# Attention and two expert layers on one core: pooling moved from GpSimd to VectorE, half tiles merged into whole ones

## The chip, the cores and the metric

The kernel runs on one core of one Trainium2 chip. A core has five engines that run at the same time, each through a list of its own in a fixed order: TensorE (PE) multiplies matrices, VectorE (DVE), ScalarE (ACT) and GpSimd (POOL) work elementwise, and SyncE (SP) issues transfers. Engines wait for each other by semaphores. PSUM is the memory that TensorE writes its products to: eight banks, of 512 float32 numbers in each of 128 partitions. SBUF is the working memory. The metric is the device time of one execution, in microseconds (us), lower is better.

## What is computed

Attention whose keys and values are averaged over groups of eight tokens, then a layer of eight experts of which each token uses one, then a second such layer with a capacity for each expert. The part that the change touches, with B = 4, H = 8, S = 576, D = 64:

```
k_p = k.reshape(B, H, Sp, pool, D).mean(axis=3)       # pool = 8, Sp = 72
v_p = v.reshape(B, H, Sp, pool, D).mean(axis=3)
scores = scale * np.matmul(q, k_p.transpose(0, 1, 3, 2))
scores = scores - np.max(scores, axis=-1, keepdims=True)
attn = np.exp(scores)
attn = attn / (np.sum(attn, axis=-1, keepdims=True) + 1e-09)
out = np.matmul(attn, v_p)                            # the tokens x of the expert layers
logits = x @ w_gate + modality_bias[modality_id]      # argmax picks the expert, softmax its weight
h = np.maximum(x[mask] @ w1[e], 0.0)                  # for each expert e
out[mask] = gate_w[mask, None] * (h @ w2[e])
```

## The kernel before

The kernel has two stages on the time line. The attention stage makes the 2304 tokens in 18 tiles of 128 tokens, nine for each of two pairs of batches, and sends each finished tile to DRAM (xs). The expert stage then gathers tokens window by window and runs the two expert layers; it is bound by products on TensorE, and the change leaves it as it is.

All orders are written by hand: each engine runs its instructions in the order in which the program text issues them. The attention stage is the loop over i at L1197. Iteration i issues, in this order: `e_trans(i-1)` (L1000, TensorE turns the exponentials of tile i-1, ScalarE copies them out as eT), `scores(i+1)` (L972), the list `steps[i]`, `exps(i+1)` (L996, ScalarE), and `values(i-1)` (L1010). Each engine therefore has the pieces of three tiles in flight, but in a fixed order.

`scores` multiplies queries and pooled keys into two PSUM tiles `sc` of four heads each; VectorE takes the row maximum of each half (L988) and subtracts it from each half (L993, into exs). `values` multiplies the turned exponentials and the pooled values into two PSUM tiles `pv`, one for each half of the heads; VectorE then makes the reciprocals rs (L1019, L1022) and scales each half into the token tile xt (L1026) and the partial logits lgh (L1030). psc and psv are pools of two one-bank buffers each, so the products of the next tile can begin on a half when VectorE has read that half.

Between these instructions stand calls of `slot()`, which issue one waiting small step of VectorE from the list `pending`: mostly the gating of three finished tiles (L164, L1034).

`steps[i]` is filled by `turn(i, ...)` (L1120): preparation for later tiles. `pool_k` and `pool_v` (L888, L891) sum eight rows of keys or values. A pair has nine blocks of 128 pooled rows, in three groups of 4, 1 and 4 blocks (GR at L843). Groups 0 and 1 of pair 0 are summed on VectorE by one reduction for two blocks (L876); all other groups are summed on GpSimd by a tree of three additions (L881, L882, L886), issued at turns 0 to 3, 8 and 9. `k_cols`, `v_cols` and `v_rows` then bring the sums into the layouts kbd and vaug, through TensorE and with copies on ScalarE and VectorE (L944, L945). `biases` (L141), 14 small VectorE instructions from L143 to L156, stands in turn 2.

In iterations 12 to 15 the class `known` (L449) prepares the first window of the first expert layer ahead of time: `choose` and `hot` (L475, L494) rank tokens and make one-hot places, `others` (L511) sums up. For the first layer these run on GpSimd (`self.eng`), for the second on VectorE. VectorE also splits the first weights there (L209).

Loads of q, k and v are issued by SP in a fixed order (L1083 to L1095 and turn 2); buffers of `kin4` and `vin4` exist twice, so the last group of a pair waits until the sums of an earlier group have been read.

Of the kernel before, what the change touches and what calls it, by code (L numbers as in the profile page):

```python
# [69 lines left out]
def build(tc, A, out):  # L70
# [378 lines left out]
    class known:  # L449
# [5 lines left out]
        def __init__(self, m, e):  # L455
            self.m, self.T = m, (T1 // 2, T2)[m - 1]
            self.g, self.e = gs[m - 1], e
            self.hs = {}
            self.eng = (G, V)[m - 1]
# [15 lines left out]
        def choose(self):  # L475

            eng = self.eng
            r, u, one = (self.part(t) for t in (kt.rk[:, :, 0], kt.rk[:, :, 1], kt.ohu[:, :, 0]))
            dn, tmp, lt, place, ohv = (self.part(t) for t in (kt.dn, kt.tmp, kt.lt, kt.place, kt.ohv))
            eng.tensor_scalar(lt, r, 128.0, None, ALU.is_ge)  # L480
            eng.tensor_scalar(place, lt, -128.0, None, ALU.mult)
            eng.tensor_tensor(place, place, r, ALU.add)
            if self.m == 2:
                eng.tensor_tensor(tmp, r, u, ALU.add)
                eng.tensor_scalar(tmp, tmp, cap, None, ALU.is_lt)
                eng.tensor_tensor(dn, tmp, one, ALU.mult)
                one = dn
            eng.tensor_scalar(tmp, r, 256.0, None, ALU.is_lt)
            eng.tensor_tensor(dn, tmp, one, ALU.mult)
            eng.tensor_tensor(tmp, dn, self.part(C(f"id{self.m}")), ALU.mult)  # L490
            eng.tensor_tensor(ohv[:, :, 1], tmp, lt, ALU.mult)
            eng.tensor_tensor(ohv[:, :, 0], tmp, ohv[:, :, 1], ALU.subtract)
# [18 lines left out]
        def others(self):  # L511
# [5 lines left out]
            self.eng.tensor_scalar(self.part(kt.offp), kt.rk[:, 0:T, 0], kt.count, -1.0, ALU.min, ALU.mult)  # L517
            self.eng.tensor_scalar(self.part(kt.offp), self.part(kt.offp), 256.0, None, ALU.add)
            self.eng.tensor_scalar(kt.count, kt.count, -1.0, 256.0, ALU.mult, ALU.add)
            self.eng.tensor_scalar(kt.more, isgs[self.m - 1], kt.count, None, ALU.mult)  # L520
            self.eng.tensor_scalar(self.part(kt.shut), dn, 64.0, None, ALU.mult)
            if T < T2:
                self.eng.tensor_copy(kt.offp[:, T:], kt.count.to_broadcast([128, T2 - T]))
                self.eng.memset(kt.shut[:, T:], 0.0)
# [294 lines left out]
    with ExitStack() as es:  # L819
# [46 lines left out]
        def pool_rows(src, dst, pair, g, eng):  # L866
# [6 lines left out]
            if eng is V:  # L873
                for i, j in [(i, min(i + 2, n)) for i in range(0, n, 2)]:
                    u = o[:, i:j, 0] if dst is kps else o[:, i:j]
                    V.tensor_reduce(u, s[:, i:j].rearrange("p t (r d) -> p t d r", r=POOL), AX.X, ALU.add)  # L876
                    if dst is kps:
                        V.tensor_copy(o[:, i:j, 1], u)
                return
            t = ld.tile([128, 4, m], F32, name="tree")[:, 0:n]  # L880
            eng.tensor_tensor(t, s[:, :, 0:m], s[:, :, m : 2 * m], ALU.add)  # L881
            eng.tensor_tensor(t[:, :, 0 : m // 2], t[:, :, 0 : m // 2], t[:, :, m // 2 : m], ALU.add)  # L882
            a, z = t[:, :, 0:D], t[:, :, D : 2 * D]
            if dst is kps:
                a, z = bc(a, 2, [128, n, 2, D]), bc(z, 2, [128, n, 2, D])
            eng.tensor_tensor(o, a, z, ALU.add)  # L886

        def pool_k(pair, g, eng):  # L888
            pool_rows(kin, kps, pair, g, eng)

        def pool_v(pair, g, eng):  # L891
            pool_rows(vin, vps, pair, g, eng)
# [59 lines left out]
        pending = []  # L952

        def slot():
            if pending:
                pending.pop(0)()

# [15 lines left out]
        def scores(tile_):  # L973
            pair, i = divmod(tile_, 9)
            ex = exs[tile_ % 3][:, 0 : H * SK].rearrange("p (h g) -> p h g", h=H)
            scs, mxs = [], []
            for half in range(2):
                sc = psc.tile([128, 4, SK], F32, name="sc")
                for j in range(2):
                    c = 2 * half + j  # L980
                    for p0, n, b in parts(tile_):
                        if i < 8:
                            q = qT[pair, i % 4][:, c, i // 4, :, :]
                        else:
                            q = qT[pair, 4][:, c, b % 2, 0, :]
                        mm(sc[p0 : p0 + n, 2 * j : 2 * j + 2, :], q, kbd[b][:, c, :], start=True, stop=True)
                mx = at.tile([128, 4], F32, name=f"mx{half}")
                V.tensor_reduce(mx, sc, AX.X, ALU.max)  # L988
                slot()
                scs.append(sc)  # L990
                mxs.append(mx)
            for half in range(2):
                V.tensor_tensor(ex[:, 4 * half : 4 * half + 4, :], scs[half], bc(mxs[half], 2, [128, 4, SK]), ALU.subtract)  # L993
                slot()
# [15 lines left out]
        def values(tile_, eT, x, lgh):  # L1010
            rs = at.tile([128, H], F32, name="rs")
            pvs = []
            for half in range(2):
                pv = psv.tile([128, 4, VA], F32, name="pv")
                for j in range(3):
                    for p0, n, b in parts(tile_):
                        mm(pv[p0 : p0 + n, j : j + 2, :], eT[:, 3 * half + j, p0 : p0 + n], vaug[b][:, half, j],  # L1017
                           start=(j == 0), stop=(j == 2), skip_group_check=True)
                V.tensor_scalar(rs[:, 4 * half : 4 * half + 4], pv[:, :, D + E], float(POOL), POOL * 1e-9, ALU.mult, ALU.add)  # L1019
                pvs.append(pv)  # L1020
            slot()
            V.reciprocal(rs, rs)  # L1022
            slot()
            for half in range(2):
                hs = slice(4 * half, 4 * half + 4)
                V.tensor_tensor(  # L1026
                    x[:, 0:DM].rearrange("p (h d) -> p h d", h=H)[:, hs, :],
                    pvs[half][:, :, 0:D], bc(rs[:, hs], 2, [128, 4, D]), ALU.mult)
                slot()
                V.tensor_tensor(lgh[:, hs, :], pvs[half][:, :, D : D + E], bc(rs[:, hs], 2, [128, 4, E]), ALU.mult)  # L1030
# [69 lines left out]
        for g in range(2):  # L1100
            pool_k(0, g, V)
# [41 lines left out]
        turn(0, pool_k, 0, 2, G)  # L1143
        turn(1, pool_v, 0, 2, G)
# [4 lines left out]
        for g in range(2):  # L1149
            turn(2, pool_k, 1, g, G)  # L1150
# [186 lines left out]
```

## Time and profile before

| | |
|---|---|
| median of 3 runs | 653.54 us (650.95 to 657.12) |
| profiled execution: its time | 657.79 us |
| profiled execution: its span | 656.0 us |
| TensorE busy | 593.5 us, 90% of the span |
| VectorE busy | 411.2 us, 63% |
| ScalarE busy | 224.8 us, 34% |
| GpSimd busy | 149.6 us, 23% |
| end of the attention stage (first product of the expert stage) | 126.97 us |
| TensorE granted clock, mean | 0.955 |

The span is what the trace covers; about 1.8 us of the execution's time lie around it. The attention stage is some 127 us of it. A busy share is a mean over stages, so the attention stage is read apart in what follows. [...] "Idle before" in a row names what the engine's next instruction waited for. A row of the time line that merges several instructions gives the start of the first and the time until the end of the last.

### The profile page before, as it was taken

How to read it: one execution, taken by the hardware profiler on the slowest of the kernel's cores; microseconds unless marked ns; L12 is line 12 of the kernel's file. 1: busy time of each engine (PE TensorE's matmuls, PEld its weight loads, DVE VectorE, ACT ScalarE, POOL GpSimd, SP SyncE). 2: the span in 40 equal slices, each digit the busy share in tenths (PEclk: the TensorE clock that was granted, in tenths of full speed). 3: DMA queues.
4: the chain of work that ended last, by engine and by line, in shares of the span. 5: the costliest groups of instructions: out<-in, count | busy, mean ns of one | idle time of the engine just before them, and what ended most of it. 6: DMA issues, size and time to landing. Idle time of an engine off the chain costs nothing. (4 is left out here: it accounts for less than half of the span.)

```text
span 656.0 us, 11642 instructions
## 1 busy us (share of the span) xinstructions
PE 593.5 (90%) x3990; PEld 531.2 (81%) x3990; DVE 411.2 (63%) x1100; ACT 224.8 (34%) x395; POOL 149.6 (23%) x149
## 2 busy tenths in 40 slices
PE   7767998889889999999999989998889999999990
PEld 4666988879788899898888878996778999988980
DVE  4689769797656867787678576227776561228110
ACT  3432674223112122112136432136663361236210
POOL 1197006012012022012113312222221212123200
PEclk8788999799979999999999989999999999999995
DMA  9997687168551022011018302926766854121110
GB/s 237 243 282 184 208 271 231 50 195 284 222 204 43 29 67 68 18 50 68 24 47 265 113 19 91 298 69 195 260 234 240 279 184 148 50 68 42 45 25 23
DMA packets 57594, 93.04 MB, mean 142 GB/s; under 512 B 6265, under 2 KB 31097, under 8 KB 57332
## 3 DMA queue, kind: packets, MB, share of 16 engines
q1 hardware_dynamic: 50084, 68.69, 33.8%
q0 software_dynamic: 7360, 22.77, 10.8%
q8 instruction: 57, 0.93, 0.6%
q14 instruction: 77, 0.63, 0.3%
q10 hardware_dynamic: 16, 0.02, 0.0%
HBM read 68.22 MB, written 24.89 MB: 142 GB/s over the span
## 5 line engine op out<-in xcount | busy, mean ns | idle before, releaser
L438 PE MATMUL py<-h,hh 128*128 128x512 f32 x296 | 119.5, 404 | 5.4 <-ACT hh L428 3.3
L398 PE MATMUL first<-xT,h 128*128 128x256 f32 x480 | 121.4, 285 | 1.4 <-issue 1.4
L399 PE MATMUL first<-xT,l 128*128 128x256 f32 x480 | 119.4, 281 | 3.2 <-issue 2.0
L439 PE MATMUL py<-l,hh 128*128 128x512 f32 x296 | 116.8, 394 | 2.2 <-DVE l L209 2.2
L440 PE MATMUL py<-h,hl 128*128 128x512 f32 x296 | 116.8, 395 | 0.0
L405 ACT ACTIVATE hh<-first 128x512 fp32r<-128x512 f32 x64 | 38.3, 598 | 211.7 <-PE first L401 196.5
L406 DVE SCALAR_TENSOR_TENSOR hl<-first,hh 128x512 fp32r<-128x512 f32 x64 | 44.2, 690 | 105.7 <-ACT hh L405 47.8
L398 PEld LDWEIGHTS first<-xT,h 128*128 128x128 f32 x480 | 91.0, 189 | 5.1 <-issue 3.6
L399 PEld LDWEIGHTS first<-xT,l 128*128 128x128 f32 x480 | 91.0, 189 | 3.5 <-DVE l L209 1.9
L209 DVE TENSOR_TENSOR l<-rr,h 128x1024 fp32r<-128x1024 f32 x72 | 83.8, 1221 | 3.4 <-ACT h L205 3.0
L736 DVE SCALAR_TENSOR_TENSOR junk<-y,wg2b 128x512 bf16<-128x512 f32 x112 | 77.3, 690 | 3.4
L401 PE MATMUL first<-xT,h 128*128 128x256 f32 x480 | 76.6, 281 | 0.0
L438 PEld LDWEIGHTS py<-h,hh 128*128 128x128 f32 x296 | 55.7, 188 | 17.9 <-ACT hh L428 6.0
L440 PEld LDWEIGHTS py<-h,hl 128*128 128x128 f32 x296 | 55.7, 188 | 13.5 <-DVE hl L413 1.1
L439 PEld LDWEIGHTS py<-l,hh 128*128 128x128 f32 x296 | 55.8, 189 | 13.0 <-DVE l L209 3.1
L401 PEld LDWEIGHTS first<-xT,h 128*128 128x128 f32 x480 | 65.5, 189 | 0.0
L205 ACT CAST h<-rr 128x1024 fp32r<-128x1024 f32 x64 | 62.8, 1044 | 2.1 <-issue 2.1
L377 POOL DMA_INDIRECT out<-y,ids x18 | 24.5, 1361 | 160.4 <-ACT y L605 107.5
L779 POOL DMA_INDIRECT ys<-y,tok x20 | 20.3, 1016 | 173.2 <-DVE y L774 101.9
L1017 PE MATMUL pv<-vaug,eT 96*128 96x146 f32 (+1 forms) x240 | 35.2, 323 | 11.6 <-DVE lgh L1030 11.6
L1017 PEld LDWEIGHTS pv<-vaug,eT 96*128 96x128 f32 (+1 forms) x240 | 32.1, 204 | 13.4 <-issue 8.8
L605 ACT ACTIVATE y<-py,xg 128x512 f32<-128x512 f32 x35 | 24.0, 686 | 38.9 <-PE py L440 28.7
(272 smaller groups left out, 888.5 us busy)
## 6 DMA issues: line engine op xcount, KB each, us to landing
rr<-in_moe_w SPq DMA_DIRECT2D x72, 512.0 KB, 6.0
ys<-zero SPq DMA_DIRECT2D x18, 260.0 KB, 6.8
xs<-xt SPq DMA_DIRECT2D x36, 130.0 KB, 2.4
out<-zero SPq DMA_DIRECT2D x1, 4608.0 KB
kin<-in_k SPq DMA_DIRECT2D x3, 1024.0 KB, 5.7
vin<-in_v SPq DMA_DIRECT2D x3, 1024.0 KB, 7.9
qin<-in_q SPq DMA_DIRECT2D x4, 512.0 KB, 11.7
wg2b<-wgd SPq DMA_DIRECT2D x1, 2048.0 KB
```

Of the source, the lines that this page charges most:

```text
L205: copy(hi[q], raw[q])
L209: eng.tensor_tensor(lo[q], raw[q], hi[q].bitcast(F32), ALU.subtract)
L398: mm(g[:, j, :], h1[q][:, c, fs], hi, start=(c == 0), stop=False)
L399: mm(g[:, j, :], l1[q][:, c, fs], hi, start=False, stop=False)
L401: mm(g[:, j, :], h1[q][:, c, fs], xT[:, c, :, 1, :], start=False, stop=(c == CH - 1))
L405: ACT.activation(hh, g, AF.Relu)
L406: V.scalar_tensor_tensor(hl, g, 0.0, hh.bitcast(F32), ALU.max, ALU.subtract)
L438: mm(py[t], hh[:, j, :], h2[q][:, j, :], start=st, stop=False)
L439: mm(py[t], hh[:, j, :], l2[q][:, j, :], start=False, stop=False)
L440: mm(py[t], hl[:, j, :], h2[q][:, j, :], start=False, stop=sp)
L736: V.scalar_tensor_tensor(junk, self.y[:, t, 0:DM], 1.0, wg2b[:, e, :], ALU.mult, ALU.mult, accum_out=self.lg[:, t, e : e + 1])
L1017: mm(pv[p0 : p0 + n, j : j + 2, :], eT[:, 3 * half + j, p0 : p0 + n], vaug[b][:, half, j], start=(j == 0), stop=(j == 2), skip_group_check ...
```

## The change

Three things change; none touches the expert stage, except that the preparation for its first window is issued on another engine.

1. `pool_rows` always runs on VectorE, by the tree of three additions, on two blocks at a time, with a `slot()` between pieces. The groups that GpSimd summed at turns 0, 1, 2, 3, 8, 9 are now summed on VectorE at turns 1, 2, 4, 5, 8, 9. Groups 0 and 1 of pair 0 use the tree too, where they used the reduction.
2. `scores` and `values` use one two-bank PSUM tile for both halves, and one VectorE instruction where there were two (maximum, subtraction, rs, xt, lgh). psc and psv have one such buffer each, so they take as many banks as before.
3. `choose`, `hot` and `others` of the first expert layer run on VectorE. On GpSimd only memsets and indirect transfers are left.

```diff
-            self.eng = (G, V)[m - 1]
...
-            if self.m == 1:
-                return [lambda t=t: G.tensor_scalar(self.ohp[:, t, :], iota, place[:, t : t + 1], None, ALU.is_equal) for t in range(T)]
-            return [lambda t=t: hot_places(self.ohp, place, t, 6) for t in range(0, T, 6)]
+            return [lambda t=t: hot_places(self.ohp, place, t, min(6, T - t)) for t in range(0, T, 6)]
...
-        psc = es.enter_context(tc.tile_pool(name="psc", bufs=2, space=PSUM))
+        psc = es.enter_context(tc.tile_pool(name="psc", bufs=1, space=PSUM))
...
-        psv = es.enter_context(tc.tile_pool(name="psv", bufs=2, space=PSUM))
+        psv = es.enter_context(tc.tile_pool(name="psv", bufs=1, space=PSUM))
...
+            for i, j in [(i, min(i + 2, n)) for i in range(0, n, 2)]:
+                t = ld.tile([128, 2, m], F32, name="tree", bufs=2)[:, 0 : j - i]
+                V.tensor_tensor(t, s[:, i:j, 0:m], s[:, i:j, m : 2 * m], ALU.add)
+                V.tensor_tensor(t[:, :, 0 : m // 2], t[:, :, 0 : m // 2], t[:, :, m // 2 : m], ALU.add)
+                a, z = t[:, :, 0:D], t[:, :, D : 2 * D]
+                if dst is kps:
+                    a, z = bc(a, 2, [128, j - i, 2, D]), bc(z, 2, [128, j - i, 2, D])
+                V.tensor_tensor(o[:, i:j], a, z, ALU.add)
+                if j < n:
+                    slot()
...
+            sc = psc.tile([128, 2, 512], F32, name="sc")[:, :, 0 : 4 * SK].rearrange("p a (h g) -> p a h g", h=4)
...
+            mx = at.tile([128, 2, 4], F32, name="mx")
+            V.tensor_reduce(mx, sc, AX.X, ALU.max)
+            slot()
+            V.tensor_tensor(ex, sc, bc(mx, 3, [128, 2, 4, SK]), ALU.subtract)
+            slot()
+            slot()
...
             slot()
+            V.tensor_scalar(rs, pv[:, :, :, D + E], float(POOL), POOL * 1e-9, ALU.mult, ALU.add)
             V.reciprocal(rs, rs)
             slot()
+            V.tensor_tensor(x[:, 0:DM].rearrange("p (a h d) -> p a h d", a=2, h=4),
+                            pv[:, :, :, 0:D], bc(rs, 3, [128, 2, 4, D]), ALU.mult)
+            slot()
+            V.tensor_tensor(lgh.rearrange("p (a h) e -> p a h e", a=2), pv[:, :, :, D : D + E], bc(rs, 3, [128, 2, 4, E]), ALU.mult)
+            slot()
...
-        turn(0, pool_k, 0, 2, G)
-        turn(1, pool_v, 0, 2, G)
+        turn(1, pool_k, 0, 2)
+        turn(2, pool_v, 0, 2)
...
-            turn(2, pool_k, 1, g, G)
-            turn(3, pool_v, 1, g, G)
+            turn(4, pool_k, 1, g)
+            turn(5, pool_v, 1, g)
...
-        turn(8, pool_k, 1, 2, G)
-        turn(9, pool_v, 1, 2, G)
+        turn(8, pool_k, 1, 2)
+        turn(9, pool_v, 1, 2)
```

The remaining lines of the diff write V for `eng` and `self.eng`, and drop the engine from the calls.

How the change moves instructions is seen in the lists of two engines. In the rows, a number behind a name is that of the buffer; line numbers of the changed kernel differ by up to 16. First VectorE from the end of tile 2's scores to the start of `biases`, before: tile 0's values (rs to lgh), then tile 3's scores.

```order
L1019 TENSOR_SCALAR rs<-pv 128x4 x2
L1022 RECIPROCAL rs<-rs 128x8
L1026 TENSOR_TENSOR xt<-pv,rs 128x256
L1030 TENSOR_TENSOR lgh<-pv,rs 128x32
L1026 TENSOR_TENSOR xt<-pv,rs 128x256
L1030 TENSOR_TENSOR lgh<-pv,rs 128x32
L988 TENSOR_REDUCE mx_423<-sc 128x4
L988 TENSOR_REDUCE mx_428<-sc 128x4
L993 TENSOR_TENSOR exs_154<-sc,mx_423 128x288
L993 TENSOR_TENSOR exs_154<-sc,mx_428 128x288
```

The same place of VectorE in the changed kernel, from the second of two equal pieces of three additions:

```order
L877 TENSOR_TENSOR tree<-kin_195 128x512
L878 TENSOR_TENSOR tree<-tree 128x2x128
L882 TENSOR_TENSOR kps<-tree 128x256
L1007 TENSOR_SCALAR rs<-pv 128x8
L1008 RECIPROCAL rs<-rs 128x8
L1010 TENSOR_TENSOR xt<-pv,rs 128x512
L1013 TENSOR_TENSOR lgh<-pv,rs 128x64
L978 TENSOR_REDUCE mx<-sc 128x8
L980 TENSOR_TENSOR exs_154<-sc,mx 128x576
```

Six additions of the last group of keys of pair 0 now stand ahead of tile 0's values, and ten instructions on halves have become six. The other groups come in the same way: `pool_v` of this group behind `biases`, and four more pairs of pieces in iterations 4, 5, 8 and 9.

The second place is VectorE in iteration 12, between tile 13's scores and tile 11's values. Before:

```order
L993 TENSOR_TENSOR exs_155<-sc,mx_1208 128x288
L993 TENSOR_TENSOR exs_155<-sc,mx_1213 128x288
L473 COPY rk<-pm 128x10
L1019 TENSOR_SCALAR rs<-pv 128x4 x2
L1022 RECIPROCAL rs<-rs 128x8
L1026 TENSOR_TENSOR xt<-pv,rs 128x256
```

The same place of VectorE in the changed kernel:

```order
L472 COPY rk<-pm 128x10
L478 TENSOR_SCALAR lt_k<-rk 128x9
L479 TENSOR_SCALAR place_k<-lt_k 128x9
L480 TENSOR_TENSOR place_k<-place_k,rk 128x9
L486 TENSOR_SCALAR tmp_k<-rk 128x9
L487 TENSOR_TENSOR dn<-tmp_k,ohu 128x9
L488 TENSOR_TENSOR tmp_k<-dn,cb 128x9
L489 TENSOR_TENSOR ohv_k<-tmp_k,lt_k 128x9
L490 TENSOR_TENSOR ohv_k<-tmp_k,ohv_k 128x9
L227 TENSOR_TENSOR ohp<-cb,place_k 128x768
L227 TENSOR_TENSOR ohp<-cb,place_k 128x384
L1007 TENSOR_SCALAR rs<-pv 128x8
```

Eight small instructions of `choose` and two of `hot` now stand ahead of tile 11's values; before they were 17 instructions on GpSimd. In iteration 15 seven instructions of `others` move over in the same way.

## Rows read from the trace of the kernel before

**Rows 1.** First line of the page.
```profile
span 656.0 us, 11642 instructions
```

**Rows 2.** Five stretches: start:end, length, busy us of PE, PEld, DVE, ACT, POOL; PEclk, DMA share, GB/s.
```profile
0.00:30.20 30.20, 21.09 (x87) 14.74 (x88) 16.61 (x29) 10.43 (x23) 2.49 (x9) 0.79 0.94 232
30.20:67.00 36.80, 26.57 (x175) 25.15 (x175) 32.60 (x95) 14.06 (x33) 30.66 (x24) 0.82 0.94 239
67.00:94.00 27.00, 26.39 (x227) 24.77 (x227) 20.63 (x95) 18.83 (x44) 0.00 (x0) 0.97 0.70 221
94.00:119.70 25.70, 20.64 (x185) 19.12 (x184) 23.48 (x95) 13.94 (x27) 13.11 (x27) 1.00 0.67 218
119.70:127.00 7.30, 7.29 (x43) 6.55 (x43) 2.81 (x16) 0.95 (x2) 0.00 (x0) 0.53 0.01 2
```

**Rows 3.** Time line, 39 to 43 us: start us, us, engine line op out<-in.
```profile
39.73 2.35 POOL L881 TENSOR_TENSOR tree<-kin 128x1024 f32<-128x1024 f32 x1
39.91 2.20 DVE L152 TENSOR_SCALAR m<-m 128x18 f32<-128x18 f32 x1
```

**Rows 4.** Groups by line and shape, VectorE, 30 to 67 us: count | busy us, mean ns | idle before.
```profile
L945 DVE COPY vaug<-cb 96x6 f32<-96x6 f32 x2 | 2.9, 1456 | 0.0
L1058 DVE TENSOR_SCALAR e<-ev 128x3 f32<-128x3 f32 x1 | 1.9, 1859 | 0.0
L1046 DVE COPY xt<-gt 128x8 f32<-128x8 f32 x3 | 1.4, 502 | 0.0
L175 DVE TENSOR_TENSOR ga_eq<-lg,ga_mx 128x24 f32<-128x24 f32 x1 | 1.1, 1071 | 0.0
```

**Rows 5.** The same groups in 67 to 127 us.
```profile
L1046 DVE COPY xt<-gt 128x8 f32<-128x8 f32 x9 | 1.1, 149 | 0.0
L1058 DVE TENSOR_SCALAR e<-ev 128x3 f32<-128x3 f32 x4 | 0.6, 159 | 0.0
L945 DVE COPY vaug<-cb 96x6 f32<-96x6 f32 x4 | 0.6, 157 | 0.0
L175 DVE TENSOR_TENSOR ga_eq<-lg,ga_mx 128x24 f32<-128x24 f32 x4 | 0.5, 132 | 0.0
```

**Rows 6.** Time line of VectorE: first row of `biases`, and the row behind its last.
```profile
36.29 1.27 DVE L143 CAST trib<-cb 128x128 bf16<-128x128 f32 x1
...
44.86 0.22 DVE L1019 TENSOR_SCALAR rs<-pv 128x4 f32<-128x4 f32 x2
```

**Rows 7.** Groups by line and shape, 0 to 185 us.
```profile
L993 DVE TENSOR_TENSOR exs<-sc,mx 128x288 f32<-128x288 f32 x36 | 15.3, 445 | 0.0
L1026 DVE TENSOR_TENSOR xt<-pv,rs 128x256 f32<-128x256 f32 x36 | 15.1, 419 | 0.2
L209 DVE TENSOR_TENSOR l<-rr,h 128x1024 fp32r<-128x1024 f32 x8 | 9.6, 1218 | 0.2 <-ACT h L205 0.2
L1030 DVE TENSOR_TENSOR lgh<-pv,rs 128x32 f32<-128x32 f32 x36 | 6.5, 180 | 0.0
L876 DVE TENSOR_REDUCE kps<-kin 128x128 f32<-128x1024 f32 x2 | 3.8, 1880 | 3.7 <-DMA kin<-in_k 3.7
```

**Rows 8.** Time line of VectorE: dependent neighbours, then independent ones.
```profile
66.21 0.17 DVE L190 TENSOR_SCALAR wrap<-rot 128x8 f32<-128x8 f32 x1
66.42 0.17 DVE L191 TENSOR_TENSOR rot<-rot,wrap 128x8 f32<-128x8 f32 x1
...
95.40 0.81 DVE L993 TENSOR_TENSOR exs<-sc,mx 128x288 f32<-128x288 f32 x2
...
134.49 3.50 DVE L209 TENSOR_TENSOR l<-rr,h 128x1024 fp32r<-128x1024 f32 x3 [0.25 <-ACT h L205]
```

**Rows 9.** Time line of TensorE: one tile's values, at 1.2 and at 2.4 GHz.
```profile
46.02 3.26 PE L1017 MATMUL pv<-vaug,eT 96*128 96x146 f32 x12 [5.25 <-DVE lgh L1030]
...
53.60 1.76 PE L1017 MATMUL pv<-vaug,eT 96*128 96x146 f32 x12
```

**Rows 10.** Time line of VectorE in iteration 0: a query copy that waits for its load.
```profile
24.27 0.43 DVE L950 COPY qr<-qin 128x512 f32<-128x512 f32 x1 [1.35 <-DMA qin<-in_q]
```

More of the change, by code (lines that the diff above doesn't have):

```diff
@@ L516, in others @@
             V.tensor_reduce(kt.count, pc, AX.X, ALU.add)
[L517 to L521, printed above, removed]
+            V.tensor_scalar(self.part(kt.offp), kt.rk[:, 0:T, 0], kt.count, -1.0, ALU.min, ALU.mult)
+            V.tensor_scalar(self.part(kt.offp), self.part(kt.offp), 256.0, None, ALU.add)
+            V.tensor_scalar(kt.count, kt.count, -1.0, 256.0, ALU.mult, ALU.add)
+            V.tensor_scalar(kt.more, isgs[self.m - 1], kt.count, None, ALU.mult)
+            V.tensor_scalar(self.part(kt.shut), dn, 64.0, None, ALU.mult)
             if T < T2:
-                self.eng.tensor_copy(kt.offp[:, T:], kt.count.to_broadcast([128, T2 - T]))
-                self.eng.memset(kt.shut[:, T:], 0.0)
+                V.tensor_copy(kt.offp[:, T:], kt.count.to_broadcast([128, T2 - T]))
+                V.memset(kt.shut[:, T:], 0.0)
             self.more, self.open, self.off = kt.more, kt.open, kt.off
@@ L864, in load_q, with slot, pool_rows @@
             qin[pair, g] = t
-        def pool_rows(src, dst, pair, g, eng):
+        pending = []
+        def slot():
+            if pending:
+                pending.pop(0)()
+        def pool_rows(src, dst, pair, g):
             t0, n = GR[g]
@@ L872, in pool_rows, with pool_k, pool_v @@
             s, m = src[pair, g], POOL // 2 * D
[L873 to L892, printed above, removed]
+            for i, j in [(i, min(i + 2, n)) for i in range(0, n, 2)]:
[8 more added lines that the diff above has]
+                    slot()
+        def pool_k(pair, g):
+            pool_rows(kin, kps, pair, g)
+        def pool_v(pair, g):
+            pool_rows(vin, vps, pair, g)
         def k_cols(pair, g):
@@ L950, in order_q @@
             eng(qr[pair, r], qin[pair, g][:, :, r - QR[g][0], :])
[L952 to L956, printed above, removed]
         qT = {}
@@ L974, in scores @@
             pair, i = divmod(tile_, 9)
[L975 to L994, printed above, removed]
+            ex = exs[tile_ % 3][:, 0 : H * SK].rearrange("p (a h g) -> p a h g", a=2, h=4)
+            sc = psc.tile([128, 2, 512], F32, name="sc")[:, :, 0 : 4 * SK].rearrange("p a (h g) -> p a h g", h=4)
+            for c in range(CH):
+                for p0, n, b in parts(tile_):
+                    if i < 8:
+                        q = qT[pair, i % 4][:, c, i // 4, :, :]
+                    else:
+                        q = qT[pair, 4][:, c, b % 2, 0, :]
+                    h = 2 * (c % 2)
+                    mm(sc[p0 : p0 + n, c // 2, h : h + 2, :], q, kbd[b][:, c, :], start=True, stop=True)
+            mx = at.tile([128, 2, 4], F32, name="mx")
[4 more added lines that the diff above has]
+            slot()
         def exps(tile_):
@@ L1100, in build @@
         for g in range(2):
-            pool_k(0, g, V)
+            pool_k(0, g)
         order_q(0, 0, V.tensor_copy)
@@ L1194, in build @@
         for g in range(2):
-            pool_v(0, g, V)
+            pool_v(0, g)
         pending += [lambda: order_q(0, 4, V.tensor_copy), lambda: order_q(0, 5, V.tensor_copy)]
```

39 lines of the change are left out of this document (14 added, 25 removed).

## The prediction

> **What bounds the kernel now.** The trace spans 656.0 us [rows 1], the execution 657.8. I read the stretches first [rows 2]. The expert stage, from 127 us on, is TensorE's, and the change moves nothing in it. So what the change is worth must be read from the first 127 us, and there the bound changes four times.
>
> Up to 30.2 us the loads decide: the transfer engines are busy 94% of the time, VectorE half. From 30.2 to 67.0 VectorE is busy 32.6 of 36.8 us and TensorE 26.6 at a mean clock of 0.82: VectorE is the bound, and GpSimd works beside it for 30.7 us. From 67 to 94 us TensorE is busy 26.4 of 27.0 and VectorE has 6.4 us to spare. From 94 to 119.7 VectorE is the bound again, 23.5 of 25.7. In the last stretch TensorE runs alone at 1.2 GHz (0.53).
>
> Then I read rows of the second stretch one by one, since 95 instructions in 32.6 us is long for such small tiles. L152, on 18 numbers for each partition, took 2.20 us; GpSimd's first addition ran from 39.73 to 42.08, and L152 ended at 42.11 [rows 3]. Four lines took 132 to 159 ns after 67 us, where GpSimd adds nothing, and up to 1859 ns before [rows 4, 5]. VectorE is being held by GpSimd's additions. What this costs: `biases` takes 44.86 - 36.29 = 8.57 us for 14 instructions [rows 6]; undisturbed they lie between 0.1 us each (independent) and 0.21 us (dependent, spacing in [rows 8]), that is 1.4 to 2.9 us, and I take 2.0, so 6.6 are waiting. The four lines add 2.6 + 1.7 + 1.0 + 0.9 = 6.2 [rows 4, 5]. Together **12.8 us** of VectorE's 32.6.
>
> **Prices on VectorE.** From 32 to 256 numbers read from PSUM the time rises from 180 to 419 ns: 1.07 ns for each number [rows 7]. With it the addition of 1024 numbers at 1218 ns becomes 0.67 us for 512, 0.40 for 256, 0.26 for 128, 0.20 for 64; the bounds for 512 are half of L209 (0.61) and L993 with 288 (0.445) plus its missing 224 numbers (0.68). A dependent instruction starts 0.04 us after its forerunner's end (66.38, 66.42); an independent one 0.08 before it: three L209 take 3.50, not 3.66 [rows 8]. A piece of two blocks thus costs 0.67 + 0.04 + 0.40 + 0.04 + 0.40 - 0.08 = 1.47 us for keys, 1.33 for values; a single block 0.92 and 0.86.
>
> **The change, stretch by stretch.**
>
> *Up to 30.2 us.* A reduction of two blocks takes 1.88 us [rows 7], so the tree saves 0.4 to 0.55 in each of four such pieces of groups 0 and 1 of pair 0; but the next steps wait for loads, so I count nothing for it (with no load in the way, 2 us). One thing does move: in iteration 0 the two subtractions of tile 1 (0.81 us, [rows 8]) stood behind a query copy that waits for its load until 24.27 [rows 10]; now the one subtraction stands ahead of that copy. Copies of vaug behind it, and the transposes that wait for them, come earlier: **-0.7**.
>
> *30.2 to 67.* Removed: 12.8 us of waiting. Added: the last groups of pair 0 (2 x 1.47 + 2 x 1.33 = 5.6) and groups 0 and 1 of pair 1 (2.94 + 0.92 + 2.66 + 0.86 = 7.4), together 13.0. The merged halves: two independent instructions on halves follow each other at the spacing 0.81 - 0.445 = 0.365 us, where 288 numbers are 0.307; a merge saves the remaining 0.06. But the maximum and the subtraction are now a dependent pair, 0.75 + 0.04 before the second may start, which eats both savings. What is left is rs, xt and lgh, 0.2 us for a tile, 1.2 for six tiles. Sum for VectorE: -12.8 + 13.0 - 1.2 = -1.0. VectorE is idle for 4.2 us here, mostly for products at the low clock; part of it fills, since the additions wait for no product, and I take a third: -1.4. Total **-2.4**, between -5.2 (all idle time filled) and -0.1 (none, and `biases` at 2.9).
>
> *67 to 94.* The last groups of pair 1 (5.6 us) go into iterations 8 and 9, less 1.2 for merges. The 6.4 us of idle time would cover it on the mean, but they lie spread over six tiles, and two get it all. Behind these additions on VectorE stand tile 7's and 8's rs, xt and lgh; TensorE's next values product waits for lgh, since there is one pv. Iteration 8 holds 1.5 (scores) + 2.9 + 1.5 (values and gating) = 5.9 us of VectorE; TensorE's share of a tile in this stretch is 26.4/6 = 4.4, and about 5 where queries are turned. I take +0.8 there and +1.1 in iteration 9, where the vaug copies stand ahead too: **+1.9**, between 0 (all covered) and 4.4 (nothing).
>
> *94 to 119.7.* `choose`, `hot` and `others` come from GpSimd: 8 dependent instructions at 0.2, 1.6; two of `hot` with 768 and 384 numbers at 1.07 ns and 0.06 us each, 1.35; seven at 0.15: 4.0 us. Less 1.2 for merges 2.8, of which VectorE's idle 2.2 us can take about one: **+1.8**, between +0.6 and +2.8. The gather of the first window starts with the copy of its rows on VectorE, behind the same work, and is not what is waited for last.
>
> *After.* Nothing. GpSimd's queue gets empty ahead of its gathers, but these wait for VectorE's row numbers, and SP's queue keeps its order; the two loads that waited for GpSimd's sums (the last groups of pair 1) now wait for VectorE's and are needed 20 us later.
>
> Sum: -0.7 - 2.4 + 1.9 + 1.8 = **+0.6 us** on 657.8, or 658.4: no change. The profiled execution lies 0.65% above the median of the runs, 653.54, so against the runs I say **654 us**.
>
> **A rule that says more.** The saving of a merge is 0.06 us by the spacing of neighbours, but 0.445 - 0.307 = 0.14 if the whole fixed part of a duration is saved. [...]
>
> **Rivals.**
>
> *A, faster: the clock stays up.* TensorE's clock fell to 1.2 GHz behind a wait of 5.25 us for lgh, and one tile's values then took 3.26 us against 1.76 [rows 9]; [rows 2] show 0.82 over the second stretch and 0.53 in the last. If shorter waits keep it at 2.4 GHz, all 4.2 us of idle time go (2.8 beyond the sum) and the last 7.3 us shrink by the factor 3.26/1.76 to 3.9 (-3.3): 0.6 - 2.8 - 3.3 = -5.5, so 648 us. Against it: the same work is done in the same 127 us, so TensorE is idle as much as before, only elsewhere.
>
> *B, slower: the clock falls more often.* Pooling in iterations 4, 5, 8 and 9 is 2.7 to 3.9 us of VectorE during which tile values wait, and TensorE with them. If the clock falls in two more places at the 3.3 us that the last stretch loses, it is 0.6 + 6.6 = +7.2, so 661 us. It decides from two falls on; one gives 657. For it: `pool_k` and `pool_v` of pair 1 come in neighbouring iterations. Against it: the worst wait now, 5.25 us, gets shorter. [...]
>
> *C, slower: the long rows were not GpSimd's doing.* Then 12.8 us stay and the additions come on top: 0.6 + 12.8, so 667. Against it stand the ends at 42.08 and 42.11 and the normal times elsewhere.
>
> *D, faster: merges save the whole fixed part.* 0.14 in each of five merges is 0.7 us for a tile instead of 0.2; over the 12 tiles in which VectorE is the bound -6, less the dependent pair's 0.1 each: -4.8 beyond the sum, so 649. Against it: neighbours overlap in [rows 8].
>
> **Chances.** Forecast 0.48 (its own range 650 to 658), A 0.17, B 0.20, C 0.04, D 0.06, smaller shifts of either sign 0.05. A measurement of this kernel tells about 1% from no change, 647.0 to 660.1. Faster by more: 0.4 of A, a third of D, a tail of the forecast: 0.12. Slower by more: half of B, C, a tail of the forecast: 0.16. Same: 0.72. The range is 647 to 661: it leaves out C, the far half of A and the far end of B.
>
> **What would show it.** Right: `biases` under 3 us, no VectorE instruction of fewer than 150 numbers over 0.4 us before 67 us, pieces of 1.3 to 1.5 us; VectorE's busy time to the end of the attention stage about as before (96 us); the first expert product at 126 to 129 us; TensorE's waits for lgh in iterations 5, 8, 9 and 12 to 15, no longer the 5.25 at 46. Wrong: an attention stage under 122 us with the clock at 1.0 after 31 us (A), over 132 us with more stretches at 0.5 (B), or long small VectorE rows without GpSimd beside them (C).

## The result and the profile after

| | before | changed |
|---|---|---|
| median of 18 runs | 655.64 us (650.95 to 657.26) | 659.20 us (656.59 to 663.50) |
| ratio, 95% interval | | 1.0065 [1.0042, 1.0087] |
| profiled execution, its span | 657.79, 656.0 us | 659.99, 658.2 us |
| first product of the expert stage | 126.97 us | 126.01 us |
| first to last product of the expert stage | 512.3 us | 514.9 us |
| last product to the end of the span | 16.7 us | 17.3 us |

The change costs 0.65%, inside the 1% that counts as no change, and is surely not a gain. A second measurement of the same kernel (e1, below) puts it at 1.1%. (Ratios leave out runs that took over 1.5% longer than the fastest of the same kernel, among them one of e3 and five of e8 with the profiled executions of both, so those two traces are not read.)

The five stretches of after, in the columns of [rows 2]:

```profile
0.00:30.20 30.20, 20.60 (x101) 15.26 (x102) 14.97 (x36) 11.31 (x25) 2.29 (x8) 0.83 0.94 234
30.20:67.00 36.80, 29.41 (x181) 26.77 (x181) 31.63 (x102) 14.21 (x35) 0.00 (x0) 0.81 0.98 242
67.00:94.00 27.00, 25.16 (x211) 23.28 (x209) 23.35 (x73) 17.83 (x41) 0.00 (x0) 0.94 0.74 238
94.00:119.70 25.70, 20.76 (x185) 19.04 (x183) 24.79 (x84) 12.69 (x23) 2.86 (x3) 1.00 0.63 195
119.70:127.00 7.30, 5.03 (x50) 4.64 (x51) 4.35 (x22) 2.30 (x6) 0.00 (x0) 1.00 0.01 3
```

GpSimd's 30.66 us in the second stretch are gone, and VectorE, which now does that work too, is busy 31.63 us there instead of 32.60. From 67 to 94 us it is busy 2.7 us longer, from 94 to 119.7 us 1.3 us.

VectorE's time line of after from the last group of keys of pair 0 to the last group of values, with `biases` between (start us, us, engine line op out<-in):

```profile
30.70 0.68 DVE L877 TENSOR_TENSOR tree<-kin 128x512 f32<-128x512 f32 x1
...
32.22 0.68 DVE L877 TENSOR_TENSOR tree<-kin 128x512 f32<-128x512 f32 x1
...
36.44 0.22 DVE L143 CAST trib<-cb 128x128 bf16<-128x128 f32 x1
...
37.40 0.18 DVE L152 TENSOR_SCALAR m<-m 128x18 f32<-128x18 f32 x1
...
38.27 0.69 DVE L877 TENSOR_TENSOR tree<-vin 128x512 f32<-128x512 f32 x1
...
39.65 0.68 DVE L877 TENSOR_TENSOR tree<-vin 128x512 f32<-128x512 f32 x1
```

`biases` takes 38.27 - 36.44 = 1.83 us where [rows 6] had 8.57; L152, 2.20 us in [rows 3], takes 0.18. The other three long lines of [rows 4], by line and shape in 30 to 67 us of after, and the maximum and the subtraction with them (count | busy us, mean ns | idle before):

```profile
L980 DVE TENSOR_TENSOR exs<-sc,mx 128x576 f32<-128x576 f32 x6 | 4.5, 756 | 0.3
L978 DVE TENSOR_REDUCE mx<-sc 128x8 f32<-128x576 f32 x5 | 3.8, 750 | 1.8 <-PE sc L976 1.8
L1030 DVE COPY xt<-gt 128x8 f32<-128x8 f32 x3 | 0.4, 150 | 0.0
L943 DVE COPY vaug<-cb 96x6 f32<-96x6 f32 x2 | 0.3, 159 | 0.0
L1042 DVE TENSOR_SCALAR e<-ev 128x3 f32<-128x3 f32 x1 | 0.2, 163 | 0.0
```

The copy for xt, the one for vaug and the step for e (L1046, L945 and L1058 of before) are down from 502, 1456 and 1859 ns to 150, 159 and 163. No small row is held any more.

TensorE's values of five tiles of after (tiles 2, 5, 10, 16 and 17), and the first expert product:

```profile
42.44 3.26 PE L1004 MATMUL pv<-vaug,eT 96*128 96x146 f32 x12
...
64.62 2.08 PE L1004 MATMUL pv<-vaug,eT 96*128 96x146 f32 x12
...
91.44 1.66 PE L1004 MATMUL pv<-vaug,eT 96*128 96x146 f32 x12
...
121.11 1.73 PE L1004 MATMUL pv<-vaug,eT 96*128 96x146 f32 x12 [2.29 <-DVE lgh L1013]
...
124.36 1.72 PE L1004 MATMUL pv<-vaug,eT 96*64 96x146 f32 x24 [0.85 <-DVE e L1042]
...
126.01 0.39 PE L398 MATMUL first<-xT_k,h 128*128 128x256 f32 x1
```

The wait of 5.25 us of [rows 9] is gone, and tile 2 starts 3.6 us earlier. Its products still run at the low clock (3.26 us at a granted clock of 0.50), which the prediction calls 1.2 GHz; the records give the clock only as a share. At the end it is the other way round: here tiles 16 and 17 run at a granted clock of 1.00 (1.73 and 1.72 us), where those of before took 3.26 at 0.50 and 2.82 at 0.59:

```profile
119.71 3.26 PE L1017 MATMUL pv<-vaug,eT 96*128 96x146 f32 x12 [2.23 <-DVE lgh L1030]
...
124.22 2.82 PE L1017 MATMUL pv<-vaug,eT 96*64 96x146 f32 x24
126.97 0.38 PE L398 MATMUL first<-xT_k,h 128*128 128x256 f32 x1
```

So the attention stage came out 1 us shorter, the expert stage, whose text the change leaves alone, 2.6 us longer. There the two traces differ in waits of TensorE, some of them behind branches of its program. The first product of L422, which stands behind such a branch (TensorE's last one ahead of it is recorded at 323.13 us in before and at 321.23 in after), of before and then of after:

```profile
324.52 0.21 PE L787 MATMUL sums<-oi,op 128*128 128x18 bf16 x2
325.90 0.71 PE L422 MATMUL first<-xT,h 128*128 128x256 f32 x4 [1.18 <-ACT y L605]
```
```profile
322.71 0.21 PE L783 MATMUL sums<-oi,op 128*128 128x18 bf16 x2
325.71 1.19 PE L422 MATMUL first<-xT,h 128*128 128x256 f32 x4 [2.79 <-issue]
```

After the same work TensorE stood for 1.18 us, and now for 2.79 us in which it waits for nothing that the profile shows; behind it the granted clock was 0.50 (1.19 us for four products against 0.71 at 1.00). Elsewhere it is the other way round. The waits that differ most, of before and then of after:

```profile
184.92 0.37 PE L399 MATMUL first<-xT,l 128*128 128x256 f32 x1 [2.04 <-issue]
...
385.81 0.37 PE L787 MATMUL sums<-oi,op 128*128 128x18 bf16 x2 [2.62 <-DVE oi L770]
```
```profile
377.94 0.36 PE L398 MATMUL first<-xT_k,h 128*128 128x256 f32 x1 [1.87 <-issue]
...
380.74 1.01 PE L401 MATMUL first<-xT_k,h 128*128 128x256 f32 x3 [1.50 <-issue]
```

The wait at 184.92 us of before has no counterpart in after. Where TensorE of before waited 2.62 us for VectorE, after has its waits of 1.87 and 1.50 us a little ahead of that product, and none at it.

### The profile page after: what moved, and what is told of

Same layout as the page of the kernel before. It is cut to its first block, busy times and chain, and to the rows that moved or that the text cites. A ratio compares the mean times of both kernels' runs of the same rounds, so it can differ in the third digit from the quotient of the medians.

```text
span 658.2 us, 11533 instructions
## 1 busy us (share of the span) xinstructions
PE 597.0 (91%) x3990; PEld 534.4 (81%) x3990; DVE 413.6 (63%) x1078; ACT 225.4 (34%) x395; POOL 110.4 (17%) x101
```

## The experiments

The theory after this result was that the attention stage does what the sum said, and that the loss comes from where TensorE's later code lies: 29 of its wait instructions are gone, because merged instructions need fewer, so everything behind lies 29 places earlier. Rivals: chance between executions; extra work on VectorE; the low clock.

### e1 and e2: both kernels again

No edit. First the changed kernel, then that of before.

> The changed kernel once more, for a second profile. In its first profile the first product of the expert stage starts at 126.0 us against 127.0 before, yet the whole is longer; the difference arises in the expert stage, at places where TensorE ran at 1.2 GHz (from 324.9 and 379.5 us) behind waits for code. Theory 1 (the loss lies in the expert stage, at such places): first product again at 125 to 127 us, ratio to before 1.004 to 1.008, low-clock stretches behind the same waits. Theory 2 (the first profile was a lucky attention stage; the loss lies in the attention stage): first product at 129 to 132 us. Theory 3 (chance of these runs): ratio 0.998 to 1.002.

> The kernel before once more, for a second profile and as a measure of what a ratio of two equal programs shows. All theories: ratio 0.998 to 1.002. Theory 1: first product of the expert stage at 126 to 128 us, and the wait at the first two-group product behind the turn from the seventh to the eighth window (1.18 us in the first profile, against 2.79 in the changed kernel) again under 2 us. Theory 2: first product at 123 to 126 us.

Ratios 1.0114 [1.0077, 1.0150] and 1.0002 [0.9974, 1.0030]. The first product of L422, of e2 and then of e1:

```profile
326.31 0.72 PE L422 MATMUL first<-xT,h 128*128 128x256 f32 x4 [1.19 <-ACT y L605]
```
```profile
327.91 1.19 PE L422 MATMUL first<-xT,h 128*128 128x256 f32 x4 [2.80 <-issue]
```

The same programs have the same waits: 1.18 and 1.19, 2.79 and 2.80. These are no chance. The attention stage is less stable: its end lies at 126.97 and 126.27 us in the two executions of before, at 126.01 and 128.51 in those of after. So e1 fits none of the theories by its numbers: its end lies between those of theories 1 and 2, its ratio above that of theory 1.

### e3 and e4: 60 tiny products ahead of the warm-up

The same lines were put into the changed kernel (e3) and into that of before (e4); they compute nothing that is used.

```diff
         pw = psm.tile([128, 4, 128], F32, name="pm")
+        for _ in range(60):
+            mm(pw[0:1, 0, 0:1], oneb[:, 0:1], oneb[:, 0:1], start=True, stop=True)
         for _ in range(14):
```

> The changed kernel with 60 tiny products of one column added to the warm-up of TensorE, where it waits for the first loads: no time in the attention stage, but all later code of TensorE lies 60 products further on. Theory 1 in the form that code loading decides: the ratio moves away from that of the changed kernel by 0.3% or more, either way, and the waits for code move to other places. Theory 2, and theory 1 in the form that only the phase of the clock decides: same ratio as the changed kernel within 0.2%.

> The kernel before with the same 60 tiny products in the warm-up. If the place of the code decides (theory 1, code loading): the ratio lies 0.3% or more from 1, either way. If not: 0.998 to 1.002, and the first product of the expert stage at 127 us in both cases.

Ratios 1.0192 [1.0145, 1.0240] and 1.0169 [1.0136, 1.0203]. In e4 the attention stage ended at 124.80 us, about 2 us earlier than before, and the expert stage took 517.6 us, 5.3 more. The new waits stand at L422 again; here the one of the last window, of before and then of e4:

```profile
465.24 0.39 PE L440 MATMUL py<-h,hl 128*128 128x512 f32 x1
465.47 0.71 PE L422 MATMUL first<-xT,h 128*128 128x256 f32 x4
```
```profile
465.52 0.39 PE L440 MATMUL py<-h,hl 128*128 128x512 f32 x1
469.01 0.71 PE L422 MATMUL first<-xT,h 128*128 128x256 f32 x4 [3.10 <-ACT y L605]
```

No wait before, 3.10 us now (put down to a ScalarE copy that had come last). Nothing but the place of the code has changed there, so the place alone can bring a wait of 3 us. In the runs of e4 the 60 products cost 1.7%, more than the whole change; its profiled execution was 4.1 us longer than that of before (661.92 and 657.79 us), 0.6%.

### e5 to e8: the parts

e5 is part 1 alone (pooling on VectorE), e6 part 2 alone (merged halves), e7 part 3 alone (`choose`, `hot`, `others` on VectorE), e8 parts 1 and 2. Each takes its lines of the diff above and leaves the others as before.

> Only the pooling part of the change: all sums on VectorE by the tree, halves unmerged, small steps of the first expert layer still on GpSimd. The prediction's terms: no VectorE rows held by GpSimd between 30 and 67 us (12.8 us less), 13.0 us more of additions there, 5.6 us more in iterations 8 and 9, 1.2 us more for each of three stretches without the merges. Theory of the terms: first product of the expert stage at 126 to 129 us. If the loss of the whole is in the attention stage and comes from pooling: 130 us or more.

> Only the merged halves. By the terms 0.2 us of VectorE for a tile less: first product of the expert stage at 124 to 127 us, ratio 0.993 to 1.002. If the merged PSUM tiles delay TensorE (one buffer, products wait for the whole tile): 128 us or more.

> Only choose, hot and others of the first expert layer on VectorE, pooling on GpSimd and halves as before. By the terms 4.0 us more of VectorE in 94 to 120 us, of which about 1 fills idle time: first product of the expert stage 1.5 to 3 us later than before (128.5 to 130), ratio 1.002 to 1.005. If hidden: 127 us.

> The change without its third part: pooling on VectorE and merged halves, small steps of the first expert layer on GpSimd as before. By the terms the changed kernel less 2 to 3 us in the attention stage: first product of the expert stage at 123 to 125 us. If the whole follows the attention stage: ratio 0.995 to 1.000; if the expert stage decides (waits for code and low clock): anywhere from 0.995 to 1.008.

| kernel | median us (runs) | ratio, interval | TensorE's program against before | start of values of tile 5, 10, 16 | first expert product | expert stage | wait ahead of first L422 |
|---|---|---|---|---|---|---|---|
| before | 655.64 (18) | | 0 | 67.46, 91.52, 119.71 | 126.97 | 512.3 | 1.18 |
| e2, before again | 654.53 (12) | 1.0002 [0.9974, 1.0030] | 0 | 67.93, 92.08, 120.25 | 126.27 | 512.9 | 1.19 |
| changed | 659.20 (18) | 1.0065 [1.0042, 1.0087] | -29 | 64.62, 91.44, 121.11 | 126.01 | 514.9 | 2.79 |
| e1, changed again | 661.45 (6) | 1.0114 [1.0077, 1.0150] | -29 | 64.63, 92.72, 122.36 | 128.51 | 513.5 | 2.80 |
| e5, part 1 | 657.78 (12) | 1.0035 [1.0004, 1.0067] | -2 | 62.6, 89.2, 117.6 | 122.15 | 513.4 | 2.81 |
| e6, part 2 | 655.72 (12) | 1.0018 [0.9985, 1.0051] | -26 | 64.2, 89.2, 118.2 | 123.04 | 512.7 | 3.18 |
| e7, part 3 | 656.10 (12) | 1.0024 [0.9993, 1.0056] | 0 | 64.1, 92.1, 121.9 | 126.50 | 513.5 | 1.41 |
| e8, parts 1, 2 | 659.80 (7) | 1.0074 [1.0027, 1.0121] | -29 | | | | |

The fourth column counts instructions in the two compiled programs; the records of the traces give the same differences. No part alone is worth much, and none is a gain in the runs. The one that lengthens the stretch from tile 10 to 16 most is part 3, as the prediction had it: 29.8 us against 28.2 before, 28.4 in e5 and 29.0 in e6. That part 2 lengthens it by 0.8 us was not foretold: with one pv, TensorE waits there for the gating (1.15 us at tile 13 of e6) and for the copy xt (1.43 us at tile 14).

e5 and e6 bring the values of tile 10 forward by 2 to 3 us and end the attention stage 3 to 5 us earlier in their profiled executions, and yet their runs are not shorter. These ends lie below what was expected of both (126 to 129 and 124 to 127 us), and that of e7, 126.50, below the 128.5 to 130 of its terms. One execution says little here: e10 and e11 below have the attention stages of e5 and e6, and there tile 10 comes at 91.92 and 90.83 us and the end at 124.69 and 126.17. Nor do the 2 to 3 us that part 3 was to cost show between e8 and the changed kernel: their ratios are 1.0074 and 1.0065.

e5 and e6 also part what held VectorE's small rows. In e6, where GpSimd still adds, `biases` takes 44.29 - 35.13 = 9.16 us and L152 2.20 us; in e5, where it doesn't, 40.01 - 38.19 = 1.82 and 0.18.

### e9 to e11: TensorE's code put back where it was

If the place of the code decides, a program that is made as long again as that of before should have its waits again. The changed kernel gets 13 tiny products ahead of the warm-up and one behind it (e9); in the records of its trace these are 15 products and 15 weight loads more and one wait less, 29 in all. e5 gets one tiny product, two instructions (e10); e6 gets 13 (e11). Here e9:

```diff
         pw = psm.tile([128, 4, 128], F32, name="pm")
+        for _ in range(13):
+            mm(pw[0:1, 0, 0:1], oneb[:, 0:1], oneb[:, 0:1], start=True, stop=True)
         for _ in range(14):
             mm(pw, oneb, bc(oneb, 1, [128, 4, 128]), start=True, stop=True)
+        mm(pw[0:1, 0, 0:1], ident[:, 0:1], ident[:, 0:1], start=True, stop=True)
```

> The changed kernel with 14 tiny products ahead of and behind the warm-up (13 of 1x1 ahead, one of 1x1 behind it that reads ident), nothing else. The changed kernel's TensorE program is 29 instructions shorter than that of before, all of them waits that the merged instructions no longer need; the 14 products with their weight loads and one more wait are 29, so everything from the attention on stands where it stood before. Theory 'the loss is where TensorE's code lies': the gap ahead of the first product of L422 goes back from 2.8 us to some 1.2, the expert stage's products from 514.9 us to some 512.5, and with the attention stage 1 us shorter than before the time is 0.997 to 1.003 of before. Rival 'the loss is a wait for data or another engine': gap, expert stage and ratio stay as in the changed kernel (2.8 us, 514 to 515 us, 1.0065). Rival 'any added products cost': ratio above 1.0065, as the 60 tiny products did.

> The pooling on VectorE alone (the rest as before) with one tiny 1x1 product ahead of the warm-up: its TensorE program was 2 instructions shorter than that of before, and is now as long. By 'where TensorE's code lies' the gap ahead of the first product of L422 goes from 2.81 us to 1.2 to 1.4, and the ratio from 1.0035 to 1.000 to 1.002. If two instructions don't matter, the gap stays at 2.8 us and the ratio at 1.0035.

> The merged halves alone (the rest as before) with 13 tiny 1x1 products ahead of the warm-up, which make up for the 26 waits that the merge took out of TensorE's program. By 'where TensorE's code lies' the gap ahead of the first product of L422 goes from 3.18 us to 1.2 to 1.4 and the ratio from 1.0018 to 0.997 to 1.000, below both kernels if anything here is. Otherwise 3.2 us and 1.002.

TensorE's time line of e9 at the three places, then the first L422 of e10:

```profile
185.24 0.37 PE L399 MATMUL first<-xT,l 128*128 128x256 f32 x1 [2.04 <-issue]
...
327.42 0.71 PE L422 MATMUL first<-xT,h 128*128 128x256 f32 x4 [1.17 <-ACT y L601]
...
388.34 0.37 PE L783 MATMUL sums<-oi,op 128*128 128x18 bf16 x2 [3.64 <-DVE oi L766]
```
```profile
325.51 0.71 PE L422 MATMUL first<-xT,h 128*128 128x256 f32 x4 [1.57 <-ACT y L605]
```

e9 has the waits of before at each of the three places: 2.04 as in before, 1.17 for 1.18, and the wait for VectorE, 3.64 for 2.62; the one that only after had (1.50 us at 380.74) is gone. In e10 two instructions bring the wait ahead of L422 from 2.81 to 1.57 us, in e11 13 products bring it from 3.18 to 1.33. This half of the theory is shown: where these waits stand, and how long they are, goes by the place of TensorE's code, to within two instructions.

The other half fell. The ratios are 1.0115 [1.0064, 1.0165] for e9, 1.0034 [1.0003, 1.0064] for e10 and 1.0057 [1.0022, 1.0091] for e11, none clear of the same kernel without the products (1.0114 in e1, 1.0035 in e5, 1.0018 in e6). In e9 the expert stage still took 514.3 us, in e10 and e11 514.3 and 514.6 (513.4 in e5, 512.7 in e6). Between the changed kernel and before, the waits that came and those that went cancel and more: +1.6 at L422, +1.5 at 380.74 and +0.5 at 377.94 (1.34 us in before), -2.0 and -2.6, together -1.0 us.

### e12: something to do in TensorE's waits

What is left is the low clock. e12 gives TensorE products to do where it waits for pooled sums.

```diff
             pk = psm.tile([128, n, 128], F32, name="pm")
+            for z in range(8):
+                mm(pk[:, z % n, :], oneb, oneb, start=True, stop=True)
...
             pv = psm.tile([D, n, 128], F32, name="pm")
+            for z in range(8):
+                mm(pv[:, z % n, :], oneb[:, 0:D], oneb, start=True, stop=True)
```

> The changed kernel with 8 bf16 products of 128 columns, whose results the transposes behind them overwrite, ahead of each of the 12 groups of transposes of pooled keys and values (L897, L929), the places at which TensorE waits for VectorE's sums (4.8 and 3.7 us of waiting in the changed kernel's attention stage). Theory 'low clock': what the attention stage loses is TensorE at 1.2 GHz; with products to do in those waits fewer or shorter stretches at 0.5 stand between 24 and 67 us (mean granted clock of 30.2 to 67 above 0.9 against 0.81 to 0.86), the first expert product comes at 122 to 125 us against 126.0 to 128.5, and the ratio falls to 0.998 to 1.005. Rival 'VectorE is the bound': the clock may rise, the first expert product stays at 126 to 128.5, the ratio at 1.006 to 1.012. Rival 'the filler is in the way': 96 products at 0.06 to 0.11 us are 6 to 11 us of TensorE, the first expert product comes at 129 or later and the ratio is above 1.012.

Ratio 1.0165 [1.0115, 1.0214]. Two stretches of e12, to be read beside those of after, and the values of tiles 10, 16 and 17 with the first expert product:

```profile
30.20:67.00 36.80, 28.98 (x217) 26.50 (x216) 31.48 (x100) 14.95 (x37) 0.00 (x0) 0.91 0.97 249
67.00:94.00 27.00, 26.08 (x241) 24.23 (x240) 24.55 (x77) 18.30 (x41) 0.00 (x0) 1.00 0.75 236
```
```profile
91.24 1.66 PE L1008 MATMUL pv<-vaug,eT 96*128 96x146 f32 x12
...
121.40 3.26 PE L1008 MATMUL pv<-vaug,eT 96*128 96x146 f32 x12 [2.29 <-DVE lgh L1017]
...
126.17 3.19 PE L1008 MATMUL pv<-vaug,eT 96*64 96x146 f32 x24 [0.23 <-DVE e L1046]
...
129.29 0.58 PE L398 MATMUL first<-xT_k,h 128*128 128x256 f32 x1
```

The clock rose, from 0.81 to 0.91 and from 0.94 to 1.00, and yet tile 10 came at 91.24 us (91.44 in after) and tile 16 at 121.40 (121.11). Up to 67 us VectorE is busy 31.48 of 36.8 us and may set the pace. Behind that the low clock did cost time in after. From the values of tile 8 to those of tile 9 TensorE has the same work in every kernel here. This stretch in before, after, e1 and e12 (columns of [rows 2]), then TensorE's wait ahead of it in after:

```profile
83.74:87.94 4.20, 4.20 (x47) 4.00 (x47) 2.53 (x10) 3.36 (x8) 0.00 (x0) 1.00 0.58 172
82.06:87.87 5.81, 5.81 (x47) 5.36 (x47) 3.90 (x10) 3.50 (x8) 0.00 (x0) 0.71 0.69 213
81.69:89.15 7.46, 7.46 (x48) 6.95 (x48) 4.09 (x11) 3.50 (x8) 0.00 (x0) 0.54 0.68 204
83.01:87.21 4.20, 4.20 (x48) 4.00 (x47) 3.81 (x10) 3.36 (x8) 0.00 (x0) 1.00 0.60 163
```
```profile
80.92 1.21 PE L957 MATMUL pm<-cb,qr 128*128 128x128 f32 x8 [1.59 <-DVE vaug L943]
```

TensorE is busy throughout in all four, and the length goes by its clock. The wait of 1.59 us was 0.28 us in before: the copies of vaug now stand behind additions on VectorE. In the five profiled executions with pooling on VectorE and no filler (after, e1, e9, e5, e10) tile 8's values take 2.56 to 3.19 us, in the six with pooling on GpSimd (before, e2, e4, e6, e7, e11) 1.72. In e12 the wait is 0.61 us and tile 8 takes 1.72 us again. What this gave, the filler took: between the values of tiles 6 and 7, where two groups of it stand with 0.61 and 0.63 us, e12 takes 6.21 us and after 5.03. So the rival 'the filler is in the way' is the one whose numbers came, and e12 doesn't say what the attention stage would take with the clock up and no filler. Behind tile 16 TensorE is alone; there the clock fell this time (0.61 from 119.7 to 127 us, where after has 1.00), and the last two tiles took 3.26 and 3.19 us instead of 1.73 and 1.72. The expert stage took 518.0 us: TensorE's program is now 157 instructions longer than before, and the wait ahead of L422 in the last window is back with 2.92 us, as in e4 with 120 more.

## Why the prediction was right, and where it was not

**Prices.** They held. A piece takes 32.22 - 30.70 = 1.52 us for keys (1.47 foretold) and 39.65 - 38.27 = 1.38 for values (1.33); `biases` 1.83 (2.0). Two subtractions on halves took 0.81 us [rows 8], one on the whole takes 0.76, so this merge saves 0.05 where 0.06 was foretold, and rival D, which needed 0.14, falls.

**The held rows** were GpSimd's doing. Without its additions L152 and the other lines of [rows 4] are down to 0.13 to 0.18 us, and e5 and e6 tell this part from the merges, so rival C is out. VectorE's busy time in that stretch went from 32.60 to 31.63, -1.0 as the sum said (-12.8 + 13.0 - 1.2). That this agrees is partly luck, since the stretch ends at 67 us and after is some 3 us further on by then: from the start of tile 0's values to that of tile 6's VectorE is busy 33.67, 33.51 and 33.59 us (after, e1, e9), where before and e2 have 35.71 and 35.05.

**The other signs.** VectorE is busy 99.1 us up to 127 us, and 98.1 and 98.2 in e1 and e9, against 96.1: 2 to 3 us more than "about as before", as the terms behind 67 us came out. TensorE's waits for lgh in 30 to 130 us, of after (us in total, times, longest us):

```profile
PE pv L1004 <- DVE lgh L1013: 3.9, 3, 2.3
PE pv L1004 <- DVE xt L1030: 1.4, 1, 1.4
PE pv L1004 <- DVE ga_sm L177: 1.3, 1, 1.3
```

In before they were 11.6 us. The 5.25 is gone, as foretold, but none of the iterations that were named waits for lgh. The three waits are those of tiles 1, 15 and 16 (0.82, 0.79 and 2.29 us), in iterations 2, 16 and 17. In iterations 5, 14 and 15 the values wait for the gating (1.35 and 0.85 us) or for the copy xt (1.43), and in iteration 9 TensorE waits for vaug (1.59).

**Stretch by stretch.** The starts of a tile's values allow the terms to be read one by one, as means of three executions with the changed attention stage (after, e1, e9) and of two of before (before, e2):

| reached | predicted shift | before | changed | measured shift |
|---|---|---|---|---|
| values of tile 5, about 67 us | -0.7 - 2.4 = -3.1 | 67.7 | 64.8 | -2.9 |
| values of tile 10, about 92 us | -3.1 + 1.9 = -1.2 | 91.8 | 92.0 | +0.2 |
| values of tile 16, about 120 us | -1.2 + 1.8 = +0.6 | 120.0 | 121.6 | +1.6 |
| first expert product | +0.6 | 126.6 | 127.2 | +0.6 |

(e9's three starts are 65.11, 91.73 and 121.37 us.) The first term fits. Tile 5 alone would be a poor sign of it, for in e7, which leaves all of this as it was, tile 5 starts at 64.1 us; but tile 6 tells the same: 69.35, 68.98 and 69.63 us (after, e1, e9) against 72.28, 72.84 and 72.82 (before, e2, e7). The second was sized too small, +3.1 for +1.9 and still under its bound of 4.4, and the wait in it was another than lgh. From tile 6 to tile 8 the changed kernel takes 12.71, 12.71 and 12.99 us, where before takes 11.46: TensorE waits for the copies of vaug behind the additions, which the prediction had only as work of VectorE ahead of lgh. From tile 8 to tile 9 it takes 5.81, 7.46 and 5.53 us for 4.20, and that is the clock, which the sum left at nothing here. The third is +1.4 for +1.8; VectorE's work from tile 10 to tile 16 rose from 25.77 to 28.56 us (before, after), the 2.8 that were foretold. That the last row agrees to a tenth is luck, since one program's executions differ by 2.5 us there, by the clock from tile 8 to 9 (5.81 us in after, 7.46 in e1) and from tile 16 on (4.90 and 6.15). In the last 7 us it was 0.53 in before [rows 2] and 1.00 in after, but 0.77 in e2 and in e1: it changes from one execution of a program to the next.

**Rival A** did not come: from 30 to 67 us the clock is 0.81 in after, where it was 0.82, and 0.94 for 0.97 from 67 to 94 us. What a higher clock there would be worth, e12 doesn't settle, since its filler takes time too. **Rival B**'s mechanism, a clock that falls where tiles wait behind pooling, came in one place, at tile 8, in every profiled execution of the changed attention stage that is read here (after, e1, e9). It cost 1.3 to 3.3 us there; B's own price was 3.3. That the measured 659.2 lies nearer to B's 661 than to 654 is luck in part all the same, since B wanted two such falls. Its price for the last stretch is about the difference that e12 shows: 129.29 - 121.40 = 7.9 us from tile 16 to the expert stage, against 126.01 - 121.11 = 4.9 in after. At tile 8 the clock is low behind the wait of 1.59 us in after (0.71 up to tile 9's values) and full behind one of 0.61 us in e12 (1.00).

**What failed: "After. Nothing."** Two parts of the 5.2 us between 654 and 659.2 can be told apart. 2.1 us are the base: three runs of before had a median of 653.54, eighteen have 655.64. (Beside e1 the base is back at 653.77 and the changed kernel at 661.45, so that there the base explains nothing.) The other 3.1 us are the term that was set to zero behind 127 us, and the step from the profiled execution to the runs. In the profiled executions the expert stage takes 514.9, 513.5 and 514.3 us (after, e1, e9) against 512.3 and 512.9, +1.6 on the mean, and the end 17.3, 17.8 and 16.7 against 16.7 and 16.7, +0.6. With +0.6 of the attention stage that is +2.8 us, or 0.4%. I had counted only work and data that the change moves past 127 us, of which there is none; but the change also takes 29 instructions out of TensorE's program, and with them the later waits move.

**What stays open.** The waits that came and went cancel, and e9, which has those of before, is no faster. The rest of the expert stage's +1.6 us goes with the low clock: two stretches in the profiled execution of before between 127 and 635 us, 10.2 us in all, four in e2 (17.0 us), five in after (23.8) and in e1 (17.0), three in e9 (17.0). That is a parallel, not a proof, and a weak one: e2 has as much low clock as e1 and e9 and takes 0.6 to 1.4 us less. No experiment set this clock by itself. And the profiled executions show 0.4% where the runs show 0.65 to 1.1%: some runs of before take 651 us, and no profile caught such a run (657.79 and 657.58 us). Where those runs are faster I can't say.

## What to carry to other kernels

When two engines hold each other up, price the work at the undisturbed rate on both sides: here 12.8 us of waiting for GpSimd were traded for 13.0 us of additions, and that was to be seen before the run. Price what the clock may do behind a new wait of TensorE: here a wait of 1.59 us for a copy was followed by a stretch that took 1.3 to 3.3 us longer at the low clock. Follow a change by milestones on the engine that sets the end (the start of each tile's values), since busy shares and a single end time mix the terms with the clock. And before a change of half a per cent is believed in either direction, a program should be timed again with a few idle instructions ahead of it: 60 of them cost 1.7% here.

## What the runs showed of the hardware

Waits that come with the place of TensorE's code are long, and the same program has them again: ahead of the first L422 1.18 and 1.19 us in before and e2, 2.79 and 2.80 in after and e1. This wait was 1.17 to 1.57 us in the six profiled executions whose TensorE program is as long as that of before (before, e2, e7, e9, e10, e11), and 2.79 to 3.18 us in those that are shorter or longer (after, e1, e4, e5, e6, e12); two instructions were enough to turn one into the other (e5 and e10). Around that product transfers run on a queue whose kind the profile names instruction. From 319 to 327 us they are these, of before and then of after (queue, kind: packets, MB, share of 16 engines):

```profile
q8 instruction: 3, 0.05, 2.2%
```
```profile
q8 instruction: 3, 0.05, 3.0%
```

Both have three packets of 16 KB there, and in after they take longer together (3.0% for 2.2%). Which engine they are for, the rows don't say. So "waits for code", as some expectations call these waits, is the author's estimate: the runs show that they go by the place of TensorE's code, not what TensorE stands still for.
